# Experts' second products by seven half-size products, with cooked weights kept in DRAM

## The chip, the cores and the metric

The kernel runs on one core of a Trainium2 chip, as one program. The metric is device time in microseconds (us). TensorE (PE) multiplies; LDWEIGHTS (PEld) brings in the stationary operand of each matmul. VectorE (DVE) and ScalarE (ACT) do the elementwise work, GpSimd (POOL) a little of it, and all DMAs of the program are issued from SyncE's queue (SP, in the trace SPq) in program order.

## The reference

Linear attention (softmax of q over its features, of k over the positions) gives a token matrix x of 2304 x 512. It goes through `((x @ w1) * (x @ w2)) @ w3 @ w_out`, then through four experts:

```python
p = domain_probs / (domain_probs.sum(-1, keepdims=True) + 1e-09)
out = np.zeros((N, D), dtype=np.float32)          # N = 2304, D = 512
for e in range(E):                                 # E = 4, F = 1024
    h = np.maximum(x @ w1[e], 0.0)                 # first product, 512 -> 1024
    out += p[:, e:e + 1] * (h @ w2[e])             # second product, 1024 -> 512
```

## The kernel before

**Three matmuls for one.** Every float32 operand is split into a rounded high part (ACT, line 101) and a rest (DVE, line 102), and a product is the sum of three matmuls: high x high, high x low, low x high (lines 106 to 108 where `mm3` issues them).

**Stages.** The middle product runs over five chunks of tokens (four of 512, one of 256). For the first chunks its weights are converted; w1 and w2 in split form are saved to DRAM (line 441) and loaded again for each later chunk (line 446, `wg<-w`). Then `w3 @ w_out` is made once (`W`), the `y` steps of chunks 0 and 1 run, and for chunks 2, 3, 4 each step f does `ab` (24 matmuls), `h`, and the `y` step (12 matmuls) of the step before. y goes to DRAM (`yd<-yt`, line 510). Attention of later batches is placed between these steps.

**The experts.** Tokens form 3 groups of 768. Each group goes through 8 blocks (4 experts, each in two halves of its 1024 inner columns), so 24 blocks, numbered n. A block has two parts:

- `layer1(n)`, the first product, is already done by one level of Strassen's scheme (Winograd's form): seven products of half-size operands, with 384 tokens as moving columns, 84 matmuls (line 811, `hp`). It needs seven token combinations (`tset`, once a group) and seven weight combinations (`e1_steps`; sums at line 609, splits at 101/102), which are made again for every block from a raw load (`load_e`, lines 557 and 560).
- `layer2(n, ...)`, the second product, is done plainly: six tiles of 128 tokens, each 4 x 3 matmuls of 512 columns, 72 matmuls (`op`). Its weights are split again for every block (`e2_split`, `e2g`), its left operand is the split result of ReLU (lines 790, 791). Each tile is then scaled by its probability and added to `acc` by one 512-wide DVE instruction (848, 852).

**What sets the order.** The code's order gives priorities, and a list scheduler puts the instructions of each engine in a fixed order, so PE may take pieces of `layer1(n + 1)` between those of `layer2(n)`. An engine executes its list in that order. SP's list is one queue for all loads and saves. Tile pools hold an instruction until a buffer is free.

Of the kernel before, what the change touches and what calls it, by code (L numbers as in the profile page):

```python
# [8 lines left out]
F32 = mybir.dt.float32  # L9
# [45 lines left out]
def linear_attention_moe_kernel(ctx: ExitStack, tc, q, k, v, w1, w2, w3, wo, dp, e1, e2, out):  # L55
# [11 lines left out]
    KR, KX = 4, S - 4 * P  # L67
    QP, QR = 64, 9
# [479 lines left out]
    eraw, ew, tok = {}, {}, {}  # L548
    NGE = 2 * E

    def load_e(n):
        e, m = n % NGE // 2, n % 2
        r1 = cr.tile([P, 2, KT, 256], F32, tag="R", name="e1r")
        r2 = cr.tile([P, 2, 2, 512], F32, tag="R", name="e2r")
        for hf in range(2):
            o = 512 * hf + 256 * m
            nc.sync.dma_start(out=r1[:, hf], in_=e1[e][:, o:o + 256].rearrange("(k p) f -> p k f", p=P))
        for hf in range(2):
            o = 512 * hf + 256 * m
            nc.sync.dma_start(out=r2[:, hf], in_=e2[e][o:o + 256, :].rearrange("(u p) f -> p u f", p=P))  # L560
        eraw["e1", n], eraw["e2", n] = r1, r2

    def tset(p):


        y = cr.tile([P, KT, 2, TC], F32, tag="yp", name="yp", bufs=1)
        nc.sync.dma_start(
            out=y, in_=yd[:, :, 2 * TC * p:2 * TC * (p + 1)].rearrange("p k (t n) -> p k t n", t=2)
        )
        b11, b12, b21, b22 = y[:, 0:2, 0], y[:, 0:2, 1], y[:, 2:4, 0], y[:, 2:4, 1]  # L570
        t = tok[p] = {}

        def part(name, src):
            t[name] = tp.tile([P, 2, 2, TC], F32R, tag="t", name="t")
            split(t[name][:, :, 0], t[name][:, :, 1], src)

        def minus(dst, x, y):
            nc.vector.tensor_tensor(out=dst, in0=x, in1=y, op=ALU.subtract)

        part("b11", b11)  # L580
        part("b21", b21)
        minus(b11, b12, b11)
        minus(b12, b22, b12)
        part("b22", b22)
        minus(b22, b22, b11)
        part("t2", b22)
        part("t1", b11)
        part("t3", b12)
        minus(b21, b21, b22)
        part("t4", b21)  # L590

    def e1_steps(n):


        r = eraw.pop(("e1", n))
        a11, a12, a21, a22 = r[:, 0, 0:2], r[:, 0, 2:4], r[:, 1, 0:2], r[:, 1, 2:4]
        w = ew[n] = {}

        def part(name, src):
            def do():  # L600
                g = (ex if n == 0 and name in ("a11", "a12") else ep).tile(
# [6 lines left out]
        def comb(dst, x, y, op):  # L608
            return lambda: nc.vector.tensor_tensor(out=dst, in0=x, in1=y, op=op)
# [294 lines left out]
```

## Time and profile before

| | |
|---|---|
| three runs | 1198.53, 1199.51, 1200.98 us; median 1199.51 |
| profiled execution | span 1196.7 us from first to last instruction; the median of the runs is 2.8 us above it |
| busy share of the span | PE 97%, LDWEIGHTS 85%, DVE 62%, ACT 41%, POOL 4% |
| granted TensorE clock | full (2.4 GHz) in all 40 slices of the page |
| DMA moved | 142.61 MB, 37% of the 16 engines' time |

Until about 200 us weights are converted and DMA is full; from 200 to 443 us the `y`, `ab` and attention steps run; from 443 us on the experts. A matmul's printed duration contains its pipeline, so the distance from one start to the next is what it costs. DVE instructions overlap a little as well: a group of several lasts less than their means together.

### The profile page before, as it was taken

The numbers are of one execution on the slowest core, as the hardware profiler recorded it, in microseconds if no ns is written. First come the engines' busy times: TensorE is split into PE (matmuls) and PEld (weight loads), VectorE is DVE, ScalarE is ACT, GpSimd is POOL, SyncE is SP. The second block draws the span as 40 slices with busy tenths as digits, with TensorE's granted clock in tenths as the row PEclk, the third lists the DMA queues.
The fourth block names the chain that finished last, engine by engine and source line by source line (L and its number), as shares of the span: only waits on it lengthen the run. The fifth ranks groups of instructions, "written<-read, shape, count | busy, mean of one in ns | idle before, by whom it ended". The sixth has DMA issues, their size and how long they took to land.

```text
span 1196.7 us, 15160 instructions
## 1 busy us (share of the span) xinstructions
PE 1165.3 (97%) x5752; PEld 1015.5 (85%) x5752; DVE 741.8 (62%) x1252; ACT 494.4 (41%) x1038; POOL 49.0 (4%) x70
## 2 busy tenths in 40 slices
PE   5889999999999999999999999999999999999998
PEld 4667888788788898889999889999988888888997
DVE  7897866312234139666667876666667766666654
ACT  4675435423332235444444544443445433343331
POOL 0022310102001000000000000000000000000000
PEclk9999999999999999999999999999999999999999
DMA  9999940053376344222222342222111411222202
GB/s 244 281 350 314 356 157 12 20 201 126 106 257 220 108 158 157 71 71 71 71 71 71 125 122 71 71 71 65 54 60 68 114 58 60 71 71 71 71 1 53
DMA packets 97848, 142.61 MB, mean 119 GB/s; under 512 B 26864, under 2 KB 64240, under 8 KB 97776
## 3 DMA queue, kind: packets, MB, share of 16 engines
q1 hardware_dynamic: 97776, 141.65, 37.1%
q8 instruction: 45, 0.74, 0.3%
q14 instruction: 27, 0.22, 0.1%
HBM read 123.81 MB, written 17.83 MB: 118 GB/s over the span
## 4 chain that ended last, share of the span: by engine, by line
PE 93%; DMA 2%; ACT 2%; DVE 2%; SPq 1%; issue 0%; ACTq 0%
PE hp L811 28%; PE op L108 11%; PE op L107 11%; PE op L106 11%; PE ab L106 6%; PE ab L107 6%; PE ab L108 6%; PE y L106 3%; PE y L108 3%; PE y L107 3%; PE kv L243 2%; PE W L106 1%; PE W L108 1%; PE W L107 1%; DMA qr<-in_q_dram 1%; PE xp L324 1%
## 5 line engine op out<-in xcount | busy, mean ns | idle before, releaser
L811 PE MATMUL hp<-t,eg 128*128 128x384 f32 x2016 | 369.6, 334 | 0.1
L811 PEld LDWEIGHTS hp<-t,eg 128*128 128x128 f32 x2016 | 352.7, 188 | 10.7 <-issue 0.4
L107 PE MATMUL op<-e2g,h 128*128 128x512 f32 x576 | 226.1, 392 | 0.0
L106 PE MATMUL op<-e2g,h 128*128 128x512 f32 x576 | 225.3, 391 | 0.0
L108 PE MATMUL op<-e2g,h 128*128 128x512 f32 x576 | 222.5, 394 | 0.1
L786 ACT ACTIVATE p<-hp 128x384 f32<-128x384 f32 x144 | 65.5, 493 | 286.5 <-PE hp L811 286.5
L852 DVE SCALAR_TENSOR_TENSOR acc<-op,prob,acc 128x512 f32<-128x512 f32 x126 | 94.3, 749 | 125.8 <-PE op L108 123.1
L102 DVE TENSOR_TENSOR eg<-e1r,eg 128x512 fp32r<-128x512 f32 x164 | 112.0, 686 | 59.1 <-ACT eg L101 58.8
L101 ACT ACTIVATE eg<-e1r 128x512 fp32r<-128x512 f32 x164 | 102.8, 631 | 85.8 <-PE hp L811 47.0
L108 PEld LDWEIGHTS op<-e2g,h 128*128 128x128 f32 x576 | 108.1, 188 | 23.4 <-DVE h L791 0.9
L107 PEld LDWEIGHTS op<-e2g,h 128*128 128x128 f32 x576 | 108.0, 188 | 20.8
L106 PEld LDWEIGHTS op<-e2g,h 128*128 128x128 f32 x576 | 108.1, 188 | 19.7
L106 PE MATMUL ab<-x,wg 128*128 128x512 f32 (+1 forms) x320 | 121.2, 380 | 3.4 <-ACT wg L101 2.7
L107 PE MATMUL ab<-x,wg 128*128 128x512 f32 (+1 forms) x320 | 119.8, 375 | 0.2 <-ACT x L345 0.2
L108 PE MATMUL ab<-x,wg 128*128 128x512 f32 (+1 forms) x320 | 119.3, 375 | 0.0
L799 DVE TENSOR_TENSOR p<-hp,p 128x384 f32<-128x384 f32 x144 | 78.6, 551 | 21.2 <-ACT p L786 19.1
L476 DVE TENSOR_TENSOR ah<-ab,ah 128x512 f32<-128x512 f32 (+1 forms) x40 | 25.4, 635 | 90.2 <-PE ab L108 84.7
L791 DVE SCALAR_TENSOR_TENSOR h<-p,h 128x384 fp32r<-128x384 f32 x144 | 76.2, 550 | 0.4
L790 ACT ACTIVATE h<-p 128x384 fp32r<-128x384 f32 x144 | 71.2, 514 | 7.6 <-DVE p L799 6.9
L106 PEld LDWEIGHTS ab<-x,wg 128*128 128x128 f32 x320 | 60.7, 191 | 14.4 <-ACT wg L101 3.5
L107 PEld LDWEIGHTS ab<-x,wg 128*128 128x128 f32 x320 | 61.0, 191 | 10.7 <-ACT x L345 1.1
L108 PEld LDWEIGHTS ab<-x,wg 128*128 128x128 f32 x320 | 61.0, 191 | 10.6 <-DVE wg L102 0.2
(97 smaller groups left out, 1262.1 us busy)
## 6 DMA issues: line engine op xcount, KB each, us to landing
wg<-w SPq DMA_DIRECT2D x64, 512.0 KB, 6.9
e1r<-in_moe_w_dram SPq DMA_DIRECT2D x48, 512.0 KB, 4.4
e2r<-in_moe_w_dram SPq DMA_DIRECT2D x48, 512.0 KB, 4.5
f<-in_moe_w_dram SPq DMA_DIRECT2D x32, 512.0 KB, 6.7
w<-wg SPq DMA_DIRECT2D x16, 512.0 KB, 8.4
qr<-in_q_dram SPq DMA_DIRECT2D x16, 288.0 KB, 8.2
yp<-yd SPq DMA_DIRECT2D x3, 1536.0 KB, 7.0
out_dram<-acc SPq DMA_DIRECT2D x36, 128.0 KB, 2.4
```

The lines of the kernel that those rows point to most:

```text
L101: i = nc.scalar.activation(out=hi, in_=src, func=ACTF.Copy)
L102: eng.tensor_tensor(out=lo, in0=src, in1=hi.bitcast(F32), op=ALU.subtract)
L106: nc.tensor.matmul(out=ps, lhsT=w_hi, rhs=r_hi, start=first, stop=False)
L107: nc.tensor.matmul(out=ps, lhsT=w_hi, rhs=r_lo, start=False, stop=False)
L108: nc.tensor.matmul(out=ps, lhsT=w_lo, rhs=r_hi, start=False, stop=last)
L476: nc.vector.tensor_tensor(out=ah, in0=pss[1][:, 0:n], in1=ah, op=ALU.mult)
L786: nc.scalar.activation(out=p, in_=src, func=ACTF.Copy)
L790: nc.scalar.activation(out=g[:, 0], in_=src, func=ACTF.Relu)
L791: nc.vector.scalar_tensor_tensor(out=g[:, 1], in0=src, scalar=0.0, in1=g[:, 0].bitcast(F32), op0=ALU.max, op1=ALU.subtract,)
L799: nc.vector.tensor_tensor(out=p, in0=src, in1=p, op=ALU.add)
L811: nc.tensor.matmul(out=o, lhsT=wl[2 * sw + kt], rhs=t[b][:, kt, st], start=new and kt == 0 and i == 0, stop=kt == 1 and i == 2, skip_group ...
L852: nc.vector.scalar_tensor_tensor(out=acc[T], in0=ps, scalar=prob[:, T, e:e + 1], in1=acc[T], op0=ALU.mult, op1=ALU.add,)
```

## The change

`layer2` is now done by seven half-size products as well (columns of the weights in two halves of 256): 7 x 3 token tiles x 2 x 3 = 126 matmuls of 256 columns (line 921 of the changed kernel) in place of 72 of 512. Its left operands are seven combinations of the ReLU blocks (`mix`: 7 splits and 4 sums of 128 x 768), and its results are gathered into `acc` in 15 pieces of 256 and 3 of 512 columns (`gather`, lines 901 and 905). ReLU is applied to whole 768-wide blocks.

Weight combinations are made once. Those of e2 for all eight half-experts and of e1 for the first two are made by the generator `cooking`, whose steps are put between the `y`, `ab` and `h` steps of chunks 0 to 3 (2 a slot, then 5 a step); each finished combination (`eo`, five buffers) is saved to DRAM (line 597). The other six of e1 are made in the first token group, used from there and saved too. All later uses load them from DRAM (line 658). `layer2(n - 1)` follows `layer1(n)`: the second product runs a block behind the first.

```diff
+    NE1, NOUT = 2, 5
-    def load_e(n):
-        ...
-        for hf in range(2):
-            nc.sync.dma_start(out=r1[:, hf], in_=e1[e][:, o:o + 256].rearrange("(k p) f -> p k f", p=P))
-        for hf in range(2):
-            nc.sync.dma_start(out=r2[:, hf], in_=e2[e][o:o + 256, :].rearrange("(u p) f -> p u f", p=P))
+    USE = {
+        "e1": ["a11", "a12", "s2", "s1", "s3", "s4", "a22"],
+        "e2": ["b11", "t1", "t2", "t3", "t4", "b22", "b21"],
+    }
+    def save_e(kind, n, name, g):
+        ewd[kind, n, name] = d = dr.tile([P, 2, 2, 256], F32, name=f"{kind}_{n}_{name}")
+        nc.sync.dma_start(out=d, in_=g.bitcast(F32))
+    def cooking(pool):
+        ...
+                    g = pool.tile([P, 2, 2, 256], F32R, tag="o", name="eo", bufs=NOUT)
+                    split(g[:, 0], g[:, 1], src)
+                    waiting.append((kind, n, name, g))
+        ask(0)
+        yield
+        for i, (kind, n) in enumerate(COOKED):
+            ask(i + 1)
+            for do in cook(kind, n, raws_e.pop(i), part_of(kind, n)):   # 7 splits, 4 sums
+                do()
+                while len(waiting) > 2:
+                    save_e(*waiting.pop(0))
+                yield
+    def load_cooked(kind, n, name):
+        g = ep.tile([P, 2, 2, 256], F32R, tag="e", name="eg")
+        nc.sync.dma_start(out=g.bitcast(F32), in_=ewd[kind, n % NGE, name])
+        ew[kind, n, name] = g
@@ y steps of chunks 0 and 1; chunks 2 and 3 @@
         slot(Y0 + i, (y_step, c, f))
+        cook_some(2)
...
             ab_step(c, f)
             h_step(c, f)
+            cook_some(3)
             ...
                 y_step(c, f - 1)
+            cook_some(2)
...
         if c == NC - 2:
-            load_e(0)
-            tset(0)
+            cook_some(200)
+            kitchen.close()
+            load_y(0)
+            for g in tset(0):
+                g()
+            ep = ctx.enter_context(tc.tile_pool(name="e", bufs=9, side="right", reuse_waits="tile"))
+            for name in USE["e1"]:
+                load_cooked("e1", 0, name)
@@ layer1 @@
+        def add(u, name, src):
+            x = a[name]
+            nc.vector.tensor_tensor(out=x[:, u], in0=src, in1=x[:, u], op=ALU.add)
+            if u:
+                nc.scalar.activation(out=x, in_=x, func=ACTF.Relu)
+    def mix(n):
+        ...
+        return [
+            part("a11", a11), part("a22", a22), minus(a22, a21, a22, ALU.add),
+            part("s1", a22), minus(a21, a11, a21), minus(a11, a22, a11),
+            part("s2", a11), part("s3", a21),
+        ], [part("a12", a12), minus(a12, a12, a11), part("s4", a12)]
-    def layer2(n, h, steps):
-        order = [3, 4, 5, 0, 1, 2]
-        for x, tt in enumerate(order):
-            ...
-            for i, (hf, u) in enumerate(((0, 0), (0, 1), (1, 0), (1, 1))):
-                mm3(ps, g[:, 0, o:o + P], g[:, 1, o:o + P], wg[:, 0], wg[:, 1], i == 0, i == 3)
+    def layer2(n, work):
+        steps = [
+            ("a11", "b11", "x"), ("s1", "t1", "z"), ("s2", "t2", "x"), ("s3", "t3", "x"),
+            ("a22", "t4", "x"), ("s4", "b22", "z"), ("a12", "b21", "z"),
+        ]
+        for k, (x, b, o) in enumerate(steps):
+            w, g = ew.pop(("e2", n, b)), h[x]
+            for i in range(3):
+                ...
+                for u in range(2):
+                    for j, (sh, sw) in enumerate(((0, 0), (0, 1), (1, 0))):
+                        nc.tensor.matmul(out=q[:, c:c + DH], lhsT=g[:, sh, u, P * i:P * i + P],
+                            rhs=w[:, sw, u], ...)
+                if k == 0:
+                    gather(i, 0, 0, DH, q[:, 0:DH], first)
+                ...                      # k = 1, 2, 3, 4: one gather of 256 columns each
+                elif k == 6:
+                    gather(i, 0, 0, DM, q, False)
+            run_some(work, k, len(steps))
-    for n in range(3 * NGE):
-        h = layer1(n)
-        layer2(n, h, e1_order(n + 1) if n + 1 < 3 * NGE else [])
+    for n in range(NN):
+        ...
+            early, late = mixed.pop(n - 1)
+            layer1(n, [get("e2", n - 1), early, ys[:2]])
+            mixed[n] = mix(n)
+            for g in late:
+                g()
+            layer2(n - 1, [get_e1(n + 1), ys[2:]])
+    layer2(NN - 1, [])
```

PE's list in one block of the experts, before: `hp` is the first product of the next block, `op` the second product, one tile of 128 tokens after the other.

```order
L106 MATMUL op_5824<-e2g_5661,h_5737 128x512
L107 MATMUL op_5824<-e2g_5661,h_5737 128x512
L108 MATMUL op_5824<-e2g_5661,h_5737 128x512
L811 MATMUL hp_5903<-t_5754,eg_5881 128x384 x6
L811 MATMUL hp_6177<-t_5745,eg_6071 128x384 x4
L811 MATMUL hp_5894<-t_5760,eg_5861 128x384 x3
L106 MATMUL op_5844<-e2g_5652,h_5622 128x512
L107 MATMUL op_5844<-e2g_5652,h_5622 128x512
L108 MATMUL op_5844<-e2g_5652,h_5622 128x512
```

PE's list in a late block, after: op_11307, op_11315 and op_11323 are the three banks that take the products of steps 0, 2, 3 and 4 (`x`), op_11333 one of the three `z`.

```order
L921 MATMUL op_11307<-eg_11216,h_11294 128x256 x6
L921 MATMUL op_11315<-eg_11216,h_11294 128x256 x6
L921 MATMUL op_11323<-eg_11216,h_11294 128x256 x6
L921 MATMUL op_11333<-eg_11274,h_11304 128x256 x6
L921 MATMUL op_11333<-eg_11292,h_11300 128x256
L921 MATMUL op_11341<-eg_11274,h_11304 128x256 x6
L921 MATMUL op_11349<-eg_11274,h_11304 128x256
L921 MATMUL op_11307<-eg_11236,h_11297 128x256 x6
```

A tile's bank is finished once before; after, an `x` bank is written, read out by DVE and written again, with the `z` pieces moved between two writes of it.

DVE's list in a block of the first token group, before: `acc` is the gather of a tile, `eg` and `e1r` the next block's weight combinations, `p` and `h` the first product's sums and splits.

```order
L852 SCALAR_TENSOR_TENSOR acc_3934<-op_4963,prob_79,acc_3934 128x512
L852 SCALAR_TENSOR_TENSOR acc_3952<-op_4980,prob_79,acc_3952 128x512
L799 TENSOR_TENSOR p_5085<-hp_5096,p_5085 128x384
L799 TENSOR_TENSOR p_5094<-hp_5107,p_5094 128x384
L102 TENSOR_TENSOR eg_5270<-e1r_5072,eg_5270 128x512
L791 SCALAR_TENSOR_TENSOR h_5104<-p_5085,h_5104 128x384
L609 TENSOR_TENSOR e1r_5072<-e1r_5072 128x512
```

DVE's list in a block of the first token group, after: `blk` are the ReLU blocks, `h` their combinations, `e1r`/`eg` the weights of the next block.

```order
L905 SCALAR_TENSOR_TENSOR acc_4462<-op_5170,prob_79,acc_4462 128x512
L577 TENSOR_TENSOR blk_5060<-blk_5041,blk_5060 128x768
L905 SCALAR_TENSOR_TENSOR acc_4492<-op_5141,prob_79,acc_4492 128x256
L577 TENSOR_TENSOR e1r_4646<-e1r_4646 128x512
L103 TENSOR_TENSOR eg_5248<-e1r_4646,eg_5248 128x512
L905 SCALAR_TENSOR_TENSOR acc_4501<-op_5149,prob_79,acc_4501 128x256
L905 SCALAR_TENSOR_TENSOR acc_4471<-op_5178,prob_79,acc_4471 128x512
L577 TENSOR_TENSOR blk_5041<-blk_4998,blk_5041 128x768
L905 SCALAR_TENSOR_TENSOR acc_4510<-op_5157,prob_79,acc_4510 128x256
```

Between two gathers there are now 768-wide sums of the blocks and 512-wide ones of the weights; PE's next write into op_5141 stands behind the gather of it.

SP's list around the end of chunk 2, before: `wg` are the weights of the middle product, `yd` its result.

```order
L446 DMA wg_2813<-w1_1_787 128x1024
L557 DMA e1r_3306<-in_moe2_w1_dram 128x4x256 x2
L560 DMA e2r_3307<-in_moe2_w2_dram 128x2x512 x2
L567 DMA yp_3312<-yd_87 128x4x768
L557 DMA e1r_3771<-in_moe2_w1_dram 128x4x256 x2
L446 DMA wg_2896<-w0_2_866 128x1024
```

SP's list at the same place, after: every `e2_..<-eo` is the save of one combination.

```order
L447 DMA wg_3075<-w1_1_787 128x1024
L597 DMA e2_4_t3_3232<-eo_3218 128x1024
L597 DMA e2_4_t2_3275<-eo_3224 128x1024
L573 DMA e2r_3269<-in_moe2_w2_dram 128x2x512 x2
L597 DMA e2_4_t4_3280<-eo_3229 128x1024
L632 DMA yp_3730<-yd_87 128x4x768
L597 DMA e2_5_b11_3285<-eo_3272 128x1024
L597 DMA e2_5_b21_3344<-eo_3277 128x1024
L597 DMA e2_5_b22_3350<-eo_3282 128x1024
L597 DMA e2_5_t1_3368<-eo_3341 128x1024
L447 DMA wg_3175<-w0_2_866 128x1024
```

Seven saves now stand between the weight loads of two steps; of the 70 saves, 26 stand ahead of chunk 1's last `yd`, 27 between that and chunk 2's, and 17 behind it.

## Rows read from the trace of the kernel before

**Rows 1.** Page, part 1: busy us (share of the span) xinstructions, by engine
```profile
PE 1165.3 (97%) x5752; PEld 1015.5 (85%) x5752; DVE 741.8 (62%) x1252; ACT 494.4 (41%) x1038; POOL 49.0 (4%) x70
```

**Rows 2.** Page, part 4: chain that ended last, shares by engine, then by line
```profile
PE 93%; DMA 2%; ACT 2%; DVE 2%; SPq 1%; issue 0%; ACTq 0%
PE hp L811 28%; PE op L108 11%; PE op L107 11%; PE op L106 11%; PE ab L106 6%; PE ab L107 6%; PE ab L108 6%; PE y L106 3%; PE y L108 3%; PE y L107 3%; PE kv L243 2%; PE W L106 1%; PE W L108 1%; PE W L107 1%; DMA qr<-in_q_dram 1%; PE xp L324 1%
```

**Rows 3.** Stretches: us, busy PE, PEld, DVE, ACT, POOL, clock, DMA share, GB/s
```profile
140.00:150.00 10.00, 10.00 (x46) 8.23 (x46) 6.82 (x11) 5.60 (x11) 2.19 (x2) 1.00 1.03 399
360.00:370.00 10.00, 10.00 (x45) 8.26 (x44) 8.51 (x15) 4.65 (x7) 2.57 (x3) 1.00 0.96 376
420.00:430.00 10.00, 10.00 (x85) 10.00 (x85) 2.18 (x6) 2.02 (x5) 0.00 (x0) 1.00 0.91 366
214.00:263.00 49.00, 48.25 (x218) 38.50 (x216) 13.05 (x31) 19.04 (x43) 3.46 (x8) 1.00 0.29 93
263.00:344.00 81.00, 80.19 (x378) 65.50 (x377) 21.30 (x49) 25.76 (x59) 9.44 (x11) 1.00 0.42 141
344.00:406.00 62.00, 62.00 (x275) 51.36 (x274) 23.53 (x35) 17.11 (x27) 6.21 (x8) 1.00 0.55 199
406.00:443.00 37.00, 37.00 (x299) 36.47 (x298) 6.80 (x16) 8.60 (x21) 0.00 (x0) 1.00 0.49 185
764.72:795.88 31.16, 31.16 (x158) 28.09 (x157) 20.72 (x36) 12.43 (x26) 0.00 (x0) 1.00 0.21 68
200.00:443.00 243.00, 241.44 (x1227) 203.41 (x1225) 71.62 (x140) 74.89 (x157) 20.32 (x27) 1.00 0.41 145
```

**Rows 4.** Chain in order of time, inside the experts: start us, us, what
```profile
764.72 9.19 PE hp L811 x53
```

**Rows 5.** Timeline of PE, matmuls of 512 and 256 columns: start us, us, what
```profile
399.70 0.39 PE L108 MATMUL ab<-x,wg 128*128 128x512 f32 x1
...
403.10 0.39 PE L108 MATMUL ab<-x,wg 128*128 128x512 f32 x1
...
422.24 0.28 PE L106 MATMUL ab<-x,wg 128*128 128x256 f32 x1
...
428.84 0.28 PE L108 MATMUL y<-h,W 128*128 128x256 f32 x1
```

**Rows 6.** Groups of DVE instructions by form: busy us, mean ns, idle before
```profile
L102 DVE TENSOR_TENSOR eg<-e1r,eg 128x512 fp32r<-128x512 f32 x162 | 110.7, 686 | 59.0 <-ACT eg L101 58.8
L852 DVE SCALAR_TENSOR_TENSOR acc<-op,prob,acc 128x512 f32<-128x512 f32 x126 | 94.3, 749 | 125.8 <-PE op L108 123.1
L799 DVE TENSOR_TENSOR p<-hp,p 128x384 f32<-128x384 f32 x144 | 78.6, 551 | 21.2 <-ACT p L786 19.1 <-PE hp L811 2.1
L578 DVE TENSOR_TENSOR yp<-yp 128x768 f32<-128x768 f32 x8 | 7.6, 952 | 0.0
```

**Rows 7.** Timeline of DVE at the experts' start, back to back
```profile
447.61 1.01 DVE L799 TENSOR_TENSOR p<-hp,p 128x384 f32<-128x384 f32 x2
...
466.14 2.49 DVE L102 TENSOR_TENSOR eg<-e1r,eg 128x512 fp32r<-128x512 f32 x4
468.55 1.41 DVE L848 TENSOR_SCALAR acc<-op,prob 128x512 f32<-128x512 f32 x2
```

**Rows 8.** Page, part 6, DMA issues: xcount, KB each, median us to landing
```profile
wg<-w SPq DMA_DIRECT2D x64, 512.0 KB, 6.9
e1r<-in_moe_w_dram SPq DMA_DIRECT2D x48, 512.0 KB, 4.4
...
w<-wg SPq DMA_DIRECT2D x16, 512.0 KB, 8.4
...
yp<-yd SPq DMA_DIRECT2D x3, 1536.0 KB, 7.0
```

**Rows 9.** Waits of SP's queue: us in total, times, longest us
```profile
SPq L446 <- PE ab L108: 41.0, 11, 7.8
```

**Rows 10.** Timeline at the end: the last DVE instruction
```profile
1192.19 0.75 DVE L852 SCALAR_TENSOR_TENSOR acc<-op,prob,acc 128x512 f32<-128x512 f32 x1 [1.97 <-PE op L108]
```

More of the change, by code (lines that the diff above doesn't have):

```diff
@@ L567, in tset, with load_y @@
+    def load_y(p):
+        y = yp_.tile([P, KT, 2, TC], F32, tag="yp", name="yp")
         nc.sync.dma_start(
@@ L573, in part @@
         def part(name, src):
[L574 to L588, printed above, removed]
@@ L625, in e1_order @@
-    def e1_order(n):
-        first, a22, sums, rest = e1_steps(n)
-        return [[first[0]], [first[1]], [a22]] + [list(x) for x in zip(sums, rest)]
+            def do():
+                t[name] = tp.tile([P, 2, 2, TC], F32R, tag="t", name="t")
+                split(t[name][:, :, 0], t[name][:, :, 1], src)
+            return do
+        return [
+            part("b11", b11), part("b21", b21),
+            minus(b11, b12, b11), minus(b12, b22, b12),
+            part("b22", b22), minus(b22, b22, b11),
+            part("t2", b22), part("t1", b11), part("t3", b12),
+            minus(b21, b21, b22), part("t4", b21),
+        ]
@@ L704, in linear_attention_moe_kernel, with cook_some @@
     conv.close()
+    kitchen = ExitStack()
+    cooks = cooking(kitchen.enter_context(tc.tile_pool(name="cook", bufs=2)))
+    next(cooks)
+    def cook_some(k):
+        for _ in range(k):
+            next(cooks, None)
     for i, (c, f) in enumerate(steps):
@@ L763, in store, with run_some, layer1 @@
             nc.sync.dma_start(out=dst[n], in_=acc[t][QP * hf:QP * hf + QP])
-    def e2_split(n):
-        r = eraw.pop(("e2", n))
-        for hf in range(2):
-            for u in range(2):
-                g = e2p.tile([P, 2, 512], F32R, tag="e2", name="e2g")
-                split(g[:, 0], g[:, 1], r[:, hf, u])
-                ew[n]["e2", hf, u] = g
-    def layer1(n):
-        w, t = ew[n], tok[n // NGE]
+    def run_some(works, k, of):
+        for work in works:
+            for g in work[len(work) * k // of:len(work) * (k + 1) // of]:
+                g()
+    def layer1(n, work):
+        t = tok[n // NGE]
         steps = [
@@ new lines, in linear_attention_moe_kernel @@
+    for n in range(NE1, NE1 + 2):
+        ask_e1(n)
+    mixed = {}
+    for n in range(NN):
+        turn = n % NGE == NGE - 1 and n + 1 < NN
+        if n % NGE == NGE - 3 and n + 3 < NN:
+            load_y(n // NGE + 1)
+        ys = tset(n // NGE + 1) if turn else []
+        if n == 0:
+            layer1(n, [get_e1(1)])
+        else:
+            early, late = mixed.pop(n - 1)
[3 more added lines that the diff above has]
+                g()
+            if n + 1 < NN:
+                layer2(n - 1, [get_e1(n + 1), ys[2:]])
+            else:
+                layer2(n - 1, [get("e2", n), mixed[n][0]])
+        if n == 0:
+            mixed[n] = mix(n)
```

253 lines of the change are left out of this document (153 added, 100 removed).

## The prediction

> **What bounds the kernel now.** I read the page first: its busy shares and the chain that ended last. TensorE is busy 97% of the span [rows 1], and of the chain 93% is its own work [rows 2]; the largest piece is the experts' first product (`hp`, 28%), the next the second product (`op`, three times 11%). Then I cut the span into stretches. From 200 us on PE is busy in nearly all of the time at the full clock of 2.4 GHz (column 1.00), DVE works a third of it and DMA 41% (last row of [rows 3]); in one block of the experts PE is busy 31.16 of 31.16 us, DVE 20.72, and DMA moves 68 GB/s [rows 3]. So time comes off only where PE gets fewer cycles, and comes back where DVE, DMA or a wait takes the bound over from it.
>
> What a matmul costs is the distance of starts, since the printed durations overlap: 384 columns 9.19/53 = 0.1734 us [rows 4]; 512 columns, fifteen steps from 399.70 to 403.10, 0.2267; 256 columns, fifty-five steps from 422.24 to 428.84, 0.1200 [rows 5]. All three are columns/2.4 GHz plus about 13.3 ns, so a narrower matmul pays that surplus more often. A block of before should take 84 x 0.1734 + 72 x 0.2267 = 30.89 us; its row says 31.16, so 0.27 us go into changes between pieces. The later stretch with 256 columns shows PEld busy all the time (420 to 430 us, [rows 3]) without a longer distance, so the weight loads still fit.
>
> **The change part by part.**
>
> PE. 72 matmuls of 512 columns go (16.32 us a block), 126 of 256 come (126 x 0.1200 = 15.12). That is 1.20 us for each of 24 blocks, 28.8 us. The first product is untouched, and I keep the 0.27 us: a block of after takes 29.96 us. This is the whole gain, since PE alone bounds a block. By the Trainium skill (TensorE: Matmul & The Clock Gate, Back-to-back issue gap) a warm matmul costs its columns at 2.4 GHz plus 2.5 ns, which would be 215.8 and 109.2 ns, 1.78 us a block and 42.7 us in all. The rows show the larger surplus at both widths, so the sum goes by the rows.
>
> DVE in the experts. Distances of back-to-back instructions are shorter than their means: (2.49 - 0.69)/3 = 0.60 us for 512 wide, 1.01 - 0.55 = 0.46 for 384, 1.41 - 0.75 = 0.66 for a gather of 512 [rows 6, 7], some 0.09 below the means. The 768-wide mean is 0.952 [rows 6], so its distance is 0.86. A gather of 256 is in no row: 256 columns less are 0.952 - 0.686 = 0.27 less, so mean 0.48 and distance 0.39. After, a block has 6 sums of 384, 11 instructions of `mix` at 768, 15 gathers of 256 and 3 of 512: by distances 2.8 + 9.5 + 5.9 + 2.0 = 20.2 us, by means 23.3. Before, the same two ways give 19.4 and 22.5 for a block's 15 splits and sums of weights, 14 of the first product and 6 gathers, and the row has 20.72, four tenths of the way. So after: 21.5 of 29.96 us, 72%, against 66% before, where PE lost nothing. I cost the blocks of the second and third group at nothing.
>
> In six blocks of the first group the e1 combinations of the next block come on top: 11 of 512, 6.6 us by distances, 7.6 by means. Then DVE has 26.8 to 30.8, at four tenths 28.4 of 29.96 us. That cover is thin, and there is a place where lateness is felt at once: bank x is written at steps 2, 3 and 4 of `layer2`, and each write waits for the gather of the one before. Between a tile's last matmul of a step and its first of the next lie 12 matmuls of the other two tiles, 1.44 us, unless `z` pieces or the first product fill in, as the order has it in part. Behind a late gather DVE has 768-wide sums (0.86). I take 0.6 us a block (about one sum too many in the way), 3.6 us; bounds 0 and 18 (the second rival). In the two blocks where the token group turns, 11 `tset` instructions of 768 come instead: 20.2 + 9.5 = 29.7 by distances, 33.8 by means, at four tenths 31.4; that is 1.5 over, 3 us for both.
>
> Loads in the experts. A block of a later group loads 14 combinations of 0.524 MB, 7.3 MB in 30 us, 245 GB/s; in the first group 7 loads, 7 saves and a raw load of 1.05 MB, 8.4 MB, 280 GB/s. The rows of a full DMA move 366 to 399 [rows 3], so this fits. Nine buffers and issues seven products ahead give each load about 13 us, where 512 KB take 4.4 to 6.9 us to land [rows 8]. Nothing; if that cover went, every product (2.1 us) would wait for one load.
>
> The cooking, from about 200 to 406 us. Its instructions are 70 splits (ACT and DVE) and 40 sums: 110 x 0.60 = 66 us of DVE, and DVE works 71.62 of 243 us there [rows 3]. That fits. DMA is the question. 70 saves of 0.524 MB and 10 raw loads of 1.05 come, three early loads of the old experts (3.1 MB) go, one `yp` of 1.6 MB comes early, and 11 cooked combinations are fetched ahead of 443 us. By the places in SP's list (26, 27 and 17 saves; 5, 4 and 1 loads), added to GB/s x time of the rows:
> the y steps, from 200 to 263 us: 4.6 + 13.6 + 5.2 = 23.4 MB in 63 us, 372 GB/s;
> chunk 2: 11.4 - 3.1 + 14.2 + 4.2 = 26.7 MB in 81 us, 330;
> chunk 3: 12.3 + 1.6 + 8.9 + 1.0 = 23.9 MB in 62 us, 385;
> chunk 4: 6.8 + 5.8 = 12.6 MB in 37 us, 341 [rows 3].
> Three stretches where DMA is full or nearly so moved 399 at a share of 1.03, 376 at 0.96 and 366 at 0.91, so 387 to 402 GB/s at a share of 1 [rows 3]. At 390 all four stages fit, the y steps and chunk 3 with 1 to 3 us to spare; at 366 chunk 3 is 3.3 us late and the y steps 0.9. I take the 366 end, 4 us, because the queue will not be kept full at every moment. Upwards the bound is the convoy of the third rival; below zero I see nothing, as no PE wait of this stage goes (PE lost 1.6 us in 243).
>
> What is queued behind a wait. A split of the cooking waits for a free `eo` buffer, that is for a save to land; behind it on ACT and DVE are `ah` and `h`, for which PE's `y` step waits. A step f of `ab` and `y` lasts 36 x 0.2267 = 8.2 us and `y` runs a step behind, so a stall of some 5 us is covered once, not in every step. A save also waits in SP's list behind weight loads that wait for PE to free their buffer: 41.0 us in 11 waits, the longest 7.8 [rows 9]. It is the same wait as before, but now saves stand behind it.
>
> The ends. At the start of the experts PE finds its first nine combinations fetched. At the end a gather of 512 is last, as before (1192.19 us, and 3.8 us from its end to the span's [rows 10]); more tiles finish together there, so I add 1 us for stores issued one after the other.
>
> Sum, in the profiled execution: 1196.7 - 28.8 + 4 + 3.6 + 3 + 1 = 1179.5; with the 2.8 us by which the median of the runs lies above the span, 1182.3, say 1182.5 us.
>
> **The rivals.**
>
> All is hidden: DMA keeps 390 GB/s and DVE its 28.4 us. Then only PE's cycles count, 1199.5 - 28.8 = 1170.7. For it: DMA has held such rates for 10 us at a time, and the scheduler spread the saves forward from chunk 3. Against it: two stages with under 3 us to spare and a DVE at 95%.
>
> DVE becomes the bound in the first group: means instead of distances and 2 us of waits on ACT and PE give 33 us a block, 3 over, in six blocks 18 us, and some 5 at each of the two turns. That eats 28 of 28.8: 1198.7 us, no change. For it: DVE waits in order, with 125.8 us of idle time ahead of the gathers and 59.0 ahead of the splits in before [rows 6], and that time is no longer free. Against it: those waits were long because DVE had nothing else.
>
> The save convoy, slower. Five `eo` buffers, of which two hold combinations whose save isn't issued, leave three on the way. 70 saves with a landing time L take 70 x L/3. At `w<-wg`'s 8.4 us [rows 8] that is 196 us, inside the 206 us from 200 to 406. From L = 8.8 on it sets the stage's length, and at 10.2 it has taken the 28.8 us back with 2.4 over. At 10.6 the stage lasts 247 us, 41 more: 1199.5 - 28.8 + 41 + 3 = 1215 us. For it: 8.4 was measured under a full DMA, which this stage will now have. Against it: much of that traffic was in small pieces; `wg` loads took 6.9, an uncrowded `e1r` 4.4 [rows 8], and a late save stops PE only through ACT's and DVE's lists.
>
> The short matmul of the page: a surplus of 2.5 ns instead of 13.3. Worked out from rows as a mechanism, the distance would have to be 0.109 for 256 columns; fifty-five in a row stand at 0.120. It would give some 1157 us; I give it 2 in 100.
>
> That the combinations aren't made once is excluded by the order: each has one save.
>
> **How the numbers follow.** Forecast (1174 to 1193 us) 54 in 100, all hidden 19, DVE bound 14, convoy 11, short matmul 2. No change within 0.2% is 2.4 us, about what can be told here: 1197.1 to 1201.9. Faster takes the forecast, all hidden, the short matmul and 5 of DVE's 14, in all 80; same 5 of DVE's and 1 of the convoy, 6; slower 4 of DVE's and 10 of the convoy, 14. The range goes from 1168, a little under all hidden, to 1203, past the no-change case, and leaves out most of the convoy.
>
> **What would show it.** Right: 256-column matmuls at 0.120 us and later blocks at about 30.0; blocks of the first group 0.3 to 1 us longer, with PE waiting for gathers; DMA above 350 GB/s from 200 to 406 us with chunk 3 a few us longer. Wrong: starts at 0.125 or more, `eo` splits that wait for DMA in every step, a first group above 32 us a block, or a wait on `eg` loads in the later groups.

## The result: 1.2% faster, with two terms of the sum far off

Four runs of the changed kernel took 1183.80 to 1189.27 us, median 1185.55; four runs of the kernel before on the same chip 1198.53 to 1200.98, median 1200.11. The ratio is 0.9883 (95% interval 0.9864 to 0.9902). The forecast of 1182.5 us was 3 us too low. The profiled run took 1184.92 us with a span of 1183.1, 13.6 less than before. A kernel's time is the median of its runs, here and below; one run of the kernel with half of its last stores from ACT's queue, which took 3923.99 us, is left out.

Page of the changed kernel, busy time by engine, then the chain that ended last:

```profile
PE 1130.7 (96%) x7048; PEld 1051.4 (89%) x7048; DVE 866.8 (73%) x1428; ACT 535.8 (45%) x982; POOL 50.5 (4%) x70
...
PE 81%; DMA 8%; DVE 5%; SPq 2%; ACT 2%; issue 1%; DVEq 0%; ACTq 0%
```

PE has lost 35 us of work against [rows 1], and its share of the chain fell from 93% [rows 2] to 81%: other engines and DMA now stand between its pieces. Where, is to be seen in the stretches (us, busy PE, PEld, DVE, ACT, POOL, clock, DMA share, GB/s), which answer to [rows 3]:

```profile
214.00:263.00 49.00, 44.14 (x193) 35.27 (x192) 38.91 (x71) 30.87 (x65) 5.83 (x8) 0.97 0.89 321
263.00:344.00 81.00, 79.98 (x376) 65.30 (x375) 46.47 (x82) 37.63 (x81) 10.98 (x11) 1.00 0.95 362
344.00:406.00 62.00, 58.80 (x259) 47.99 (x258) 37.03 (x58) 25.46 (x46) 5.50 (x8) 1.00 0.96 363
406.00:443.00 37.00, 35.97 (x239) 33.13 (x238) 11.49 (x21) 10.19 (x22) 0.00 (x0) 1.00 0.92 344
443.00:480.00 37.00, 32.96 (x218) 32.76 (x217) 6.86 (x13) 10.34 (x22) 0.00 (x0) 0.95 0.66 238
510.00:690.00 180.00, 177.74 (x1259) 176.32 (x1258) 166.06 (x276) 94.77 (x153) 0.00 (x0) 1.00 0.78 278
750.00:900.00 150.00, 150.00 (x1067) 150.00 (x1066) 108.80 (x179) 60.66 (x93) 0.00 (x0) 1.00 0.74 251
```

The later groups (last row) are as drawn up: PE without a gap, DVE at 73%. The losses are in the rows above it. The chain inside the experts, which answers to [rows 4, 5]:

```profile
793.37 11.62 PE op L921 x99
804.98 1.74 PE hp L847 x10
806.73 1.41 PE op L921 x12
808.14 5.58 PE hp L847 x32
...
822.82 11.62 PE op L921 x99
```

A block takes 822.82 - 793.37 = 29.45 us instead of 31.16, so 1.71 less, 41.0 us in 24 blocks. A 256-column matmul costs 11.62/99 = 0.1174 us. With the starts of PE's matmuls as marks, the 13.6 us of the span are made up so:

| place (marks) | forecast | measured |
|---|---|---|
| PE's own work in 24 blocks | -28.8 | -41.0 |
| up to 120 us, where PE's order is the same (a mark at 118.9 is at 121.7) | 0 | +2.8 |
| y steps (last `y` of chunk 1: 262.7, now 270.8) | +0.9 | +5.3 |
| chunks 2 and 3 (last `ab` of chunk 3: 403.1, now 415.5) | +3.3 | +4.3 |
| chunk 4 (first `hp`: 443.4, now 461.4) | 0 | +5.6 |
| experts (first `hp` to last `op`: 748.4, now 713.3) | +6.6 | +5.9 |
| after the last `op` (4.9, now 8.4) | +1 | +3.5 |

The 2.8 us are a difference between executions: in the kernels below, the same mark lies between 118.7 and 123.1. Lateness of a mark is given below against the kernel before, and net of this difference.

PE's two longest waits from 190 to 290 us (us in total, times, longest), then what ends the first of them, in the chain in order of time (start, us, what):

```profile
PE xp L325 <- ACT bd L256: 3.4, 1, 3.4
PE y L108 <- DVE h L103: 1.4, 1, 1.4
```

```profile
229.90 6.81 DMA e_s<-eo
...
236.81 0.64 ACT eo L102
...
238.19 4.81 DMA e_t<-eo
243.00 0.03 ACTq L102
243.05 0.29 ACT bd L256
...
243.81 2.21 PE xp L325 x4
```

PE's matmul `xp` needs `bd` of the attention, and `bd` stands in ACT's list behind splits of the cooking (`eo`); the chain passes through two saves that land. But ACT and DVE are also at work right up to `bd`: its factor `rs` stands on DVE behind a split of 1.32 us, and on ACT a split starts 0.52 us ahead of `bd` (DVE, then ACT):

```profile
241.19 1.32 DVE L103 TENSOR_TENSOR eo<-e1r,eo 128x512 fp32r<-128x512 f32 x1 [0.28 <-ACT eo L102]
242.43 0.15 DVE L252 RECIPROCAL rs<-rs 128x1 f32<-128x1 f32 x1
```

```profile
242.53 0.61 ACT L102 ACTIVATE eo<-e1r 128x512 fp32r<-128x512 f32 x1
243.05 0.61 ACT L256 ACTIVATE bd<-kv,rs 64x64 f32<-64x64 f32 x2
```

So the chain alone doesn't tell whether the saves or the work delay `bd`. In chunk 4 the chain shows another cause:

```profile
428.10 8.56 DMA eg<-e_a
436.72 11.53 DMA wg<-w
448.30 0.38 PE ab L107
448.68 0.13 PE ab L108
448.81 0.21 PE ab L109
```

Nine `eg` loads for the experts stand in SP's list ahead of three pairs of `wg` loads for chunk 4. The page's landing times rose with the full DMA, against [rows 8]:

```profile
wg<-w SPq DMA_DIRECT2D x64, 512.0 KB, 9.4
...
e_t<-eo SPq DMA_DIRECT2D x32, 512.0 KB, 7.5
e_b<-eo SPq DMA_DIRECT2D x24, 512.0 KB, 8.6
```

### The profile page after: what moved, and what is told of

Read it like the earlier page. It is cut to its first block, busy times and chain, and to the rows that moved or that the text cites. A ratio compares the mean times of both kernels' runs of the same rounds, so it can differ in the third digit from the quotient of the medians.

```text
span 1183.1 us, 18802 instructions
## 1 busy us (share of the span) xinstructions
PE 1130.7 (96%) x7048; PEld 1051.4 (89%) x7048; DVE 866.8 (73%) x1428; ACT 535.8 (45%) x982; POOL 50.5 (4%) x70
## 4 chain that ended last, share of the span: by engine, by line
PE 81%; DMA 8%; DVE 5%; SPq 2%; ACT 2%; issue 1%; DVEq 0%; ACTq 0%
PE hp L847 29%; PE op L921 27%; PE ab L107 5%; PE ab L109 4%; PE ab L108 4%; DMA kr<-in_k_dram 2%; PE y L108 2%; PE y L107 2%; PE y L109 2%; DVE acc L905 1%; DMA eg<-e_a 1%; PE kv L244 1%; PE W L107 1%; PE W L108 1%; PE W L109 1%
## 5 line engine op out<-in xcount | busy, mean ns | idle before, releaser
L921 PE MATMUL op<-eg,h 128*128 128x256 f32 x3024 | 377.5, 280 | 1.4 <-DMA eg<-e_b 1.3
L921 PEld LDWEIGHTS op<-eg,h 128*128 128x128 f32 x3024 | 371.5, 188 | 1.9 <-issue 1.6
L905 DVE SCALAR_TENSOR_TENSOR acc<-op,prob,acc 128x256 f32<-128x256 f32 (+1 forms) x396 | 196.5, 525 | 45.8 <-PE op L921 45.4
L102 ACT ACTIVATE h<-blk 128x768 fp32r<-128x768 f32 x168 | 137.8, 842 | 142.7 <-DVE blk L577 108.8
L103 DVE TENSOR_TENSOR h<-blk,h 128x768 fp32r<-128x768 f32 x168 | 157.1, 949 | 26.9 <-ACT h L102 26.9
L830 ACT ACTIVATE blk<-hp 128x384 f32<-128x384 f32 x192 | 91.2, 490 | 147.7 <-PE hp L847 145.6
L834 DVE TENSOR_TENSOR blk<-hp,blk 128x384 f32<-128x384 f32 x144 | 79.5, 555 | 69.8 <-PE hp L847 67.5
L836 ACT ACTIVATE blk<-blk 128x768 f32<-128x768 f32 x72 | 60.8, 846 | 74.1 <-DVE blk L834 72.3
L577 DVE TENSOR_TENSOR blk<-blk 128x768 f32<-128x768 f32 x96 | 91.2, 950 | 0.6
L109 PEld LDWEIGHTS ab<-x,wg 128*128 128x128 f32 x320 | 61.7, 193 | 11.7 <-DVE wg L103 1.3
L103 DVE TENSOR_TENSOR eo<-e2r,eo 128x512 fp32r<-128x512 f32 x56 | 39.2, 706 | 40.7 <-ACT eo L102 40.7
L108 PE MATMUL y<-h,W 128*128 128x512 f32 (+1 forms) x160 | 58.4, 372 | 3.3 <-DVE h L103 3.3
L109 PE MATMUL y<-h,W 128*128 128x512 f32 (+1 forms) x160 | 57.7, 371 | 0.0
L107 PE MATMUL y<-h,W 128*128 128x512 f32 (+1 forms) x160 | 52.0, 373 | 1.0 <-ACT h L102 1.0
```

Source lines behind the costliest of these rows:

```text
L102: i = nc.scalar.activation(out=hi, in_=src, func=ACTF.Copy)
L103: eng.tensor_tensor(out=lo, in0=src, in1=hi.bitcast(F32), op=ALU.subtract)
L107: nc.tensor.matmul(out=ps, lhsT=w_hi, rhs=r_hi, start=first, stop=False)
L108: nc.tensor.matmul(out=ps, lhsT=w_hi, rhs=r_lo, start=False, stop=False)
L109: nc.tensor.matmul(out=ps, lhsT=w_lo, rhs=r_hi, start=False, stop=last)
L830: nc.scalar.activation(out=block(name)[:, u], in_=src, func=func)
```

## The experiments

Theory A: the saves cost the time, as bandwidth (A1) or because splits wait for them (A2, the convoy). Theory B: ACT and DVE instructions that PE needs stand behind the cooking's. C to H are on single places. A list scheduler orders every kernel anew, so most edits also move some other pieces.

Three traces show how far the marks move by themselves. The kernel with stores from two queues has PE's, ACT's, DVE's and POOL's instructions in the order of the changed kernel, and the two with late `eg` loads and without making combinations run PE's in that order up to 442 and 481 us. Yet in these four the y steps end 5.3, 6.2, 6.2 and 7.6 us late, at granted clocks of 0.97, 0.93, 0.93 and 0.90 from 214 to 263 us, with nearly the same wait for `bd` (3.0 to 3.4 us); chunks 2 and 3 take 144.7 to 146.3 us. So one trace of each kernel doesn't tell a difference of some 2 us in a mark.

Ratios are to the kernel before, with the 95% interval; the changed kernel has 0.9883 (0.9864 to 0.9902).

**Saves left out, work kept.**

```diff
                     split(g[:, 0], g[:, 1], src)
-                    waiting.append((kind, n, name, g))
+                    if n == 0:
+                        waiting.append((kind, n, name, g))
...
-        nc.sync.dma_start(out=g.bitcast(F32), in_=ewd[kind, n % NGE, name])
+        nc.sync.dma_start(out=g.bitcast(F32), in_=ewd.get((kind, n % NGE, name)) or ewd[kind, 0, name])
```

> Left out: the cooking makes all its combinations as before, but only those of block 0 are saved (56 of 70 saves of 0.524 MB go); later blocks load block 0's, so the loads of the experts are unchanged. In the changed kernel the experts' first product starts at 461.4 us, 18.0 later than before the change (443.4), and 12.4 of these are there at the end of chunk 3. Theory A (the transfers of the saves: a full queue, and splits that wait for a save to land): without them chunk 3 ends within 4 us of the kernel before, hp starts at 447 to 453 us, and the time falls by 8 to 14 us to 1172 to 1178. Theory B (the ACT and DVE work of 110 instructions in the way of the attention's and of h): all of that work is still there, so chunk 3 still ends 10 us or more late and the time stays within 3 us of 1185.5.

1175.66 us, ratio 0.9814 (0.9782 to 0.9846). The time and the first `hp` (450.0 us) are those of theory A, but chunk 3 ends 8.2 us late, between the two. The y steps end 8.3 us late, no better; but chunks 2 and 3 take 140.4 us from the last `y` of chunk 1 to the last `ab`, as before (140.4), where the changed kernel needs 144.7; chunk 4 takes 38.8 instead of 45.9. So the saves cost the 4.3 us of chunks 2 and 3 and, by what they push back, chunk 4. The y steps stay open, since block 0's 14 saves lie in them.

In chunks 2 and 3 the saves don't reach PE through its weights. The changed kernel's longest PE waits between 285 us and chunk 4, both gone here, are for `h` and `ah`:

```profile
PE y L108 <- DVE h L103: 1.9, 1, 1.9
PE ab L107 <- ACT ah L476: 1.3, 1, 1.3
```

**Work left out, saves kept.** Blocks other than 0 save one tile again and again.

```diff
-            for do in cook(kind, n, raws_e.pop(i), part_of(kind, n)):
-                do()
+            if n:
+                raws_e.pop(i)
+            for x in range(11) if n else cook(kind, n, raws_e.pop(i), part_of(kind, n)):
+                if n == 0:
+                    x()
+                elif x in SAVED:
+                    waiting.append((kind, n, USE[kind][SAVED.index(x)], keep[0]))
```

> Left out: the splits and sums of the cooking for all but block 0; the 56 saves stay, of one and the same tile, so that no save waits for a split and no split for a save (that tile takes one of the five eo buffers). Theory A1 (bandwidth: the queue is full): the same bytes move, so chunk 3 still ends 8 to 12 us later than in the kernel before and the time stays at 1181 to 1187. Theory A2 (the convoy: ACT and DVE stand at a split that waits for a save to land, with the attention's and h's instructions behind it) and theory B (their work): both are gone, so chunk 3 ends within 5 us of the kernel before and the time is 1173 to 1179.

1202.87 us, ratio 1.0031 (1.0019 to 1.0043): slower than everything, which no theory expected. In the y steps PE's first wait for `bd` fell from 3.4 to 1.3 us although the saves went on; that speaks for B there. Its longest PE wait between 250 and 345 us, and its stretch:

```profile
PE ab L107 <- DMA wg<-w: 14.6, 1, 14.6
...
263.00:344.00 81.00, 57.27 (x245) 43.77 (x244) 14.19 (x34) 20.80 (x46) 9.21 (x11) 0.83 1.03 396
```

With nothing to wait for, the saves fill DMA from 214 us on (395 GB/s to 263 us, then 396), and the next chunk's weights come 14.6 us late. In the changed kernel it is the splits that pace the saves. SP's longest waits in the changed kernel from 200 to 470 us, which answer to [rows 9]:

```profile
SPq L597 <- DVE eo L103: 79.6, 39, 8.2
```

The wait of a save for its split is thus also a brake that protects PE's loads. Whether the limit of five buffers is part of that brake isn't shown: a sixth, next, costs nothing.

**Six buffers, one unsaved combination.**

```diff
-    NE1, NOUT = 2, 5
+    NE1, NOUT = 2, 6
...
-                while len(waiting) > 2:
+                while len(waiting) > 1:
```

The pool `tok` opens one chunk later, for room.

> Six eo buffers instead of five, and one combination instead of two waits unsaved, so five instead of three saves can be on the way; nothing is left out. Theory A2 (convoy): the waits of eo splits for a landing save (7.9 us of ACT's in the profile) go, and chunk 3 ends 5 to 9 us earlier, the time is 1177 to 1181. Theory A1 (bandwidth) and theory B (work): chunk 3 ends within 3 us of where it did (415.5 us), the time stays within 3 us of 1185.5.

1180.60 us, ratio 0.9847 (0.9829 to 0.9866). The time lies in A2's range, but chunk 3 ends 9.8 us late against 9.6: the convoy as a bound falls. Within that, chunks 2 and 3 take 143.0 instead of 144.7, the y steps end later (7.2 against 5.3), neither clear of the spread above. The time fell through chunk 4 (42.8 instead of 45.9) and the quicker start of this execution.

**`eg` loads behind chunk 4's weights.** The seven loads move into chunk 4's step 6, and each is held, in order only, behind the last `wg` load.

```diff
+        if kind == "e1" and n < NE1:
+            hold("dma", i)
```

> The loads of block 0's and block 1's first-product combinations stand behind the last wg load of chunk 4 in SP's list instead of nine of them ahead of three pairs; nothing is left out. Theory C (those nine loads hold up chunk 4: PE waits 4 us for wg, then falls to the lower clock, 6 us lost between chunk 3's end and hp's start, and more at op 0): chunk 4 takes 38 to 41 us instead of 46, hp starts at 454 to 457 instead of 461.4, and the time falls by 4 to 7 us to 1178.5 to 1181.5. Rival D (the queue is simply behind; the eg loads are then late instead): hp starts at 460 to 463 and waits for eg, and the time is within 2 us of 1185.5.

1178.29 us, ratio 0.9829 (0.9813 to 0.9846). From chunk 3's last `ab` to the first `hp` it takes 40.1 us (45.9; before 40.3). Its stretch:

```profile
443.00:480.00 37.00, 36.15 (x248) 35.86 (x247) 12.84 (x21) 13.63 (x28) 0.00 (x0) 1.00 0.82 302
```

PE is busy 36.15 of 37 us and the clock stays at 1.00. Theory C holds, D falls: the other order gives back the whole loss of chunk 4. It took the saves too: without them the nine loads were issued at 309 to 320 us instead of 428 to 435, and the old order cost nothing (38.8 us).

**First group without making combinations.**

```diff
         if n >= NGE or n < NE1:
             return get("e1", n)
+        return [lambda name=name: load_cooked("e1", n, name) for name in USE["e1"]]
...
-    for n in range(NE1, NE1 + 2):
-        ask_e1(n)
```

> Left out: the first group makes no first-product combinations for blocks 2 to 7; it loads those of blocks 0 and 1 again, as later groups load theirs. That takes 11 DVE and 7 ACT instructions, a raw load and 7 saves from each of six blocks and puts 7 loads in. In the changed kernel the second products of blocks 0 to 8 take 240.7 us, 5.2 more than eight blocks of 29.44. Theory E (DVE in the first group costs PE these 5.2 us): the same stretch takes 235 to 237 us, the time falls by 4 to 6 us to 1179.5 to 1181.5. Rival F (it is the order in which the first group's products are interleaved, or the eg loads behind a queue still full from chunk 4): the stretch still takes 239 us or more, the time stays within 2.5 us of 1185.5.

1181.03 us, ratio 0.9830 (0.9808 to 0.9851). Blocks 0 to 8 take 237.2 us instead of 240.7. That looks like theory E. The kernel after the next one corrects it.

**No saves at all up to chunk 3.** As the first experiment, with `n == NGE - 1` in place of `n == 0`.

> Left out: only the last cooked block's combinations are saved (7 of 70 saves), and all loads read those; so from 200 us to the end of chunk 3 there is no save at all, while ACT and DVE do all the cooking's work. In all kernels run so far with the cooking's first 14 saves in place, the y steps end at 268.7 to 270.8 us against 262.7 before the change. Theory B (ACT and DVE: h and the attention's bd stand behind splits and sums, PE waits 1.4 and 3.4 us for them, and then runs its next matmuls at the lower clock): the y steps still end at 268 us or later, and chunk 3 at 409 or later. Theory A (saves: a split waits 2.3 us for a save to land, which delays bd): the y steps end at 262.5 to 265 us. The time is 1165 to 1170 by A and 1171 to 1176 by B.

1179.01 us, ratio 0.9810 (0.9788 to 0.9833), above the ranges of both theories. The y steps end 11.8 us late. PE's waits from 190 to 290 us:

```profile
PE xp L325 <- ACT bd L256: 5.8, 1, 5.8
PE kv L244 <- DVE x L103: 1.7, 1, 1.7
PE y L108 <- DVE h L103: 1.4, 1, 1.4
```

Without a single save the wait for `bd` grew from 3.4 to 5.8 us, since the unhindered splits come earlier and fill ACT's and DVE's lists (DVE 47.44 of 49 us from 214 to 263). Theory B has the y steps, A falls there.

**Six buffers and late loads together.** Both diffs above.

> Six eo buffers with one unsaved combination, and the eg loads of blocks 0 and 1 behind chunk 4's last wg load, together; nothing is left out. If the two gains are of separate places (chunk 3's end and chunk 4), the time is 1174 to 1177 us; if the six buffers only shifted the same slack (their gain also showed in chunk 4), it is that of the late loads alone, 1177.5 to 1180.

1174.11 us, ratio 0.9778 (0.9760 to 0.9796): the gains add up. And blocks 0 to 8 take 237.2 us here too, with all combinations made. The stretch of the first group, first without making them, then with both edits:

```profile
510.00:690.00 180.00, 180.00 (x1281) 180.00 (x1280) 137.65 (x223) 77.12 (x118) 0.00 (x0) 1.00 0.77 256
```

```profile
510.00:690.00 180.00, 180.00 (x1285) 180.00 (x1284) 165.93 (x278) 93.71 (x150) 0.00 (x0) 1.00 0.79 283
```

At 165.93 of 180 us DVE costs PE nothing. In the changed kernel, with 166.06, blocks 0 to 8 took 3.5 us more. So the amount of DVE work isn't the cause, and theory E falls in its simple form. F's own sign, 239 us or more without the making, did not come either. Part is one late `eg` load at the turn of the group: PE waits 1.7 us for it in the changed kernel and 0.2 in the same order with stores from two queues, where blocks 0 to 8 take 239.2 us. That the rest is the order of the lists is argued, not shown.

**Cooking held behind `h` and `bd`.** On top of both edits.

```diff
-        split(h[:, 0, 0:n], h[:, 1, 0:n], prods[c, f // 2][:, f % 2, 0:n])
+        gate["h"] = split(h[:, 0, 0:n], h[:, 1, 0:n], prods[c, f // 2][:, f % 2, 0:n])
...
-                    split(g[:, 0], g[:, 1], src)
+                    for x in split(g[:, 0], g[:, 1], src):
+                        hold("h", x)
+                        hold("bd", x)
```

> As the kernel with both edits, but the cooking's splits and sums are put in ACT's and DVE's lists only behind the h splits and the attention's bd that the code has before them, so that they no longer run ahead into the first y steps; nothing is left out, and the saves are as many. Theory B (critical ACT and DVE work stood behind cooking): PE's waits for h, ah and bd in the y steps and chunk 3 go, the y steps end at 263 to 266 us instead of 270, chunk 3 at 404 to 409, and the time falls a further 4 to 9 us below the kernel with both edits. Theory A1 (the transfers as such are the limit): the work only comes later, chunk 3 ends no earlier or the cooking runs into chunk 4, and the time is within 2 us of the kernel with both edits or above it.

1172.95 us, ratio 0.9774 (0.9741 to 0.9807). Its y steps:

```profile
214.00:263.00 49.00, 48.25 (x217) 38.54 (x215) 31.70 (x62) 28.54 (x61) 4.97 (x8) 1.00 0.78 288
```

PE is busy 48.25 of 49 us, as before the change [rows 3], with DMA at 288 GB/s (321 in the changed kernel: some saves have moved with the work). They end 0.0 us late, and with the kernel without saves this shows theory B for the y steps, waits and low clock alike. But chunks 2 and 3 still take 144.6 us, and the cooking runs into chunk 4, where 2 us are lost. The time is 1.2 us below the kernel with both edits, less than either interval: A1's case, not the 4 to 9 us of B's.

**The same in the y steps alone.** `gate` is set only for chunks 0 and 1 and the attention's batches up to the third.

> Both edits (six buffers, late eg loads) with the cooking's work held behind the h splits and the attention's bd in the y steps alone; in chunks 2 and 3 it may run ahead again. Nothing is left out. If the 7 us that the y steps gave back were lost in chunks 3 and 4 by late cooking, they stay now: the experts' first product starts at 446 to 450 us instead of 451.6, the time is 1167 to 1171. If the transfers set the end of chunk 3 however the work is placed, hp starts at 451 us or later and the time stays at 1171 to 1175.

1174.10 us, ratio 0.9790 (0.9776 to 0.9805). Net of this execution's late start (4.2 us) the first `hp` stands at 446.6 us, where the kernel with both edits has 453.9: the 7 us of the y steps now stay up to there, as the first case has it (chunks 2 and 3 take 144.7 us, chunk 4 only 39.2). But the time didn't follow, and lies in the second case's range. From the first `hp` to the last `op` of block 0 it takes 51.3 us instead of 45.6: the experts start earlier, and PE then waits 3.2 us for their `eg` loads, at a granted clock of 0.91 from 443 to 480 us. Part of the slack was shifted to the next queue, part went to the clock: with all edits, below, in the same order, the wait is 3.0 us, the clock 1.00, and it takes 48.5 us.

**Half of the last stores from ACT's queue.** On the changed kernel.

```diff
-            nc.sync.dma_start(out=dst[n], in_=acc[t][QP * hf:QP * hf + QP])
+            q = nc.scalar if t >= 12 and hf else nc.sync
+            q.dma_start(out=dst[n], in_=acc[t][QP * hf:QP * hf + QP])
```

> The changed kernel with one edit: of the last token group's stores, each tile's second half is issued from ACT's queue instead of SP's; nothing is left out. In the changed kernel the last matmul starts at 1174.7 us and the span ends 8.4 us later (4.9 before the change), with twelve stores issued one behind the other for 7.56 us. Theory G (the issue of twelve stores from one queue sets the end): the span ends 5 to 6 us after the last matmul, the time falls by 2 to 3.5 us to 1182 to 1183.5. Rival H (DVE's last gathers set it): the end stays within 1 us of 8.4 us behind the last matmul, the time within 1.5 us of 1185.5.

1182.58 us, ratio 0.9857 (0.9837 to 0.9877), which overlaps the changed kernel's; the traces decide. The stores of the changed kernel, then of this one (SP's and ACT's queue):

```profile
1172.76 7.56 SPq L807 DMA_DIRECT2D out_dram<-acc  x12
```

```profile
1172.52 4.36 SPq L808 DMA_DIRECT2D out_dram<-acc  x6
```

```profile
1172.52 5.31 ACTq L808 DMA_DIRECT2D out_dram<-acc  x6
```

The span ends 6.7 us after the last matmul instead of 8.4, outside both forecasts. Theory G has half of what was lost; the rest isn't settled.

**All edits.** Six buffers, late loads, cooking held in the y steps, stores from two queues.

> All the edits in one kernel: six buffers, late eg loads, cooking held back in the y steps, half of the last stores from ACT's queue; nothing is left out. If the gains of separate places add up: 2 to 3.5 us below the same kernel without the edit to the stores, 1165 to 1169 us, against 1199.5 before the change and 1185.5 after it.

1170.42 us, ratio 0.9763 (0.9746 to 0.9779), above the forecast of 1165 to 1169: the kernel without the stores' edit had taken 1174.10, not the 1167 to 1171 expected of it. The edit of the stores again shortens the end by 1.8 us.

**And raw loads behind block 0's second-product loads.**

```diff
             layer1(n, [get("e2", n - 1), early, ys[:2]])
+            if n == 1:
+                for m in range(NE1, NE1 + 2):
+                    ask_e1(m)
...
-    for n in range(NE1, NE1 + 2):
-        ask_e1(n)
```

They are also held, in order only, behind the last of those loads.

> As the kernel with all the edits, and the four raw first-product loads of blocks 2 and 3 (4 x 0.524 MB) stand behind block 0's second-product loads in SP's list instead of ahead of them; nothing is left out. In the kernel with all the edits PE waits 3.0 us for those loads before its first second product (3.37 us between the last hp start and the first op start). If the four raw loads are what makes them late, that wait falls under 1 us and the time by 2 to 3 us to 1167 to 1169. If the loads wait for free eg buffers (nine, held by the first product), the wait stays, and the raw loads, now later, delay the first combinations made in the first group: 1170 to 1173 us.

1164.80 us (five runs, 1163.95 to 1168.23), ratio 0.9709 (0.9695 to 0.9723): 34.8 us under the kernel before and 20.8 under the changed one, by medians. PE's wait of 3.0 us for `eg` before the first second product is gone; a later wait of 0.5 for a gather came. The time is below the first case's 1167 to 1169. The traces account for some 2 to 3 of the 5.6 us between the two medians; the rest is not explained.

## Why the prediction was right, and where its sum was not

**PE, -28.8, measured -41.0: mis-sized.** The mechanism was right. I took 72 x 0.2267 and kept 0.27 us a block for "changes between pieces". By [rows 3, 4] the second product of before really cost (31.16 - 84 x 0.1734)/72 = 0.2304 us a matmul: the 0.27 belonged to it, and went with it nearly all. That is 0.18 us a block. (In the trace the mean from one `op` to the next in that block is 0.230 us.) The 0.1200 of chunk 4 [rows 5] was also too long for the experts: 126 x (0.1200 - 0.1174) = 0.33. Together 0.51 x 24 = 12.2 us. The distances came from rows of other stages, while the block's own row held the answer. By the rule of the Trainium skill for a single, isolated matmul (TensorE: Matmul & The Clock Gate, Back-to-back issue gap) the gain would have been 42.7 us. That is near, but its distances (0.1092 and 0.2158) are not the measured ones: the surpluses, 10.7 ns on 126 matmuls and 17.1 ns on 72, happen to cancel.

**The cooking, +4, measured +15.2: two mechanisms missing.** For chunks 2 and 3 the size was about right (3.3, measured 4.3), and without saves it went; but it came as waits for `ah` and `h`, not as weights that a full DMA brings late. The failed step is "a stall of some 5 us is covered once": I applied it to `ah` and `h` and forgot the attention, whose `bd` has no such cover, and I counted DVE's and ACT's work there as fitting because their shares were low. The order of a list matters, not the share: 3.4 us for `bd`, 1.4 for `h`, and then the lower clock. The other step is "PE finds its first nine combinations fetched", true, at the price of chunk 4's weights behind them in the same queue: 5.6 us. The convoy at L = 8.8 us did not decide: `e_b` landed in 8.6, and with the sixth buffer chunk 3 ended no earlier.

**The experts, +3.6 and +3, measured 5.9.** DVE's share was right (forecast 72%, measured 108.80/150 = 73%; in the first group forecast 95%, measured 92%). The groups of after bear out the estimate of 0.48 for a narrow gather:

```profile
L103 DVE TENSOR_TENSOR h<-blk,h 128x768 fp32r<-128x768 f32 x168 | 157.1, 949 | 26.9 <-ACT h L102 26.9
L905 DVE SCALAR_TENSOR_TENSOR acc<-op,prob,acc 128x256 f32<-128x256 f32 x324 | 148.0, 477 | 45.8 <-PE op L921 45.4
```

The 3.5 us of the first group are the size forecast (3.6) by luck: with as much DVE work they went in the kernel with both edits, and part of them was a late load. The second turn costs no DVE time: it takes 32.92 + 25.92 = 58.84 us for two blocks, twice 29.45 being 58.90. In place of the 3 us for the turns came the wait of the first second product (1.3) and small ones.

**The end, +1, measured +3.5.** Right in kind, too small: all twelve stores are issued within 7.56 us, eight of them behind the last matmul, where before they were spread over 13.57 us and two came behind it:

```profile
1180.50 13.57 SPq L763 DMA_DIRECT2D out_dram<-acc  x12
```

Of the signs I had named, right were blocks without a gap in the later groups (29.45 rather than 30.0), no start at 0.125, and no `eo` split that waits for DMA in every step (ACT waited 10 times, 11.7 us in all). Blocks of the first group were 0.6 us longer (240.7/8 = 30.1), though PE waited there for a gather once only, 0.5 us. The starts at 0.120 came in chunk 4 alone, and DMA stayed under 350 GB/s in the y steps (321), where PE lost most. The total was close by luck: an error of 12 us in PE's gain and one of 11 in the cooking have opposite signs.

## What to carry to other kernels

Take a matmul's cost from the block that will be changed, as its length less its other parts over its count, not from a cleaner stretch elsewhere. For each piece of background work ask not whether its engine has time but which instruction stands behind it in that engine's list and in the DMA queue, and hold it behind those PE needs: five small edits to order, buffers and queues gave more (20.8 us, some 3 of them unexplained) than the change itself (14.6). Work that holds a transfer back can be the brake that keeps a queue free for others: take it away, and the transfers crowd out the loads that matter.

## What the runs showed of the hardware

At the same granted clock of 1.00, 256-column matmuls start 0.1200 us apart in chunk 4 of both kernels and 0.1174 in the experts. No run explains it.

After PE's wait of 4.0 us in chunk 4 sixteen 256-column matmuls start 0.21 us apart (448.81 on, above), the 1.2 GHz level; the granted clock from 445 to 455 us is 0.83. That adds about 1.5 us (16 x 0.093) to the wait. In the kernel with both edits seven 512-column matmuls at 0.43 follow the wait for `bd`.

Two 512-wide sums of DVE took 3.16 us where two others take 1.40, while POOL ran a product (DVE, then POOL, of the changed kernel):

```profile
216.88 3.16 DVE L577 TENSOR_TENSOR e1r<-e1r 128x512 f32<-128x512 f32 x2
...
230.83 1.40 DVE L577 TENSOR_TENSOR e2r<-e2r 128x512 f32<-128x512 f32 x2
```

```profile
217.14 2.36 POOL L300 TENSOR_TENSOR qe<-qe,qs 128x1152 f32<-128x1152 f32 x1 [27.70 <-DVE qs L299]
```

The `h` split behind them is the one for which PE waits 1.4 us, less than the 1.76 that the two sums took longer. The split of 1.32 us ahead of `bd`, above, where others take 0.69, falls into a POOL product as well (240.12 to 242.81 us). By the Trainium skill (SBUF — State Buffer, SBUF: two separate sides) a DVE instruction with two SBUF inputs and a GpSimd instruction that reads SBUF hold a shared pair of ports one at a time; the rows agree, though no run here separates it from another cause.
